# The first W1 quarter ahead of phi, keys, values and queries, and one order for the first softmax, the first VW and the first W2 chunks

## The chip, the cores and the metric

The kernel runs on one core of one Trainium2 chip. The metric is the device time of one execution in microseconds (us); a smaller time is better. The kernel before was timed in three runs.

## The reference

Three stages follow each other, all in float32, over 8 batches of 576 rows and 512 columns. An attention over 32 memory slots per head comes first, then a layer norm with a two-layer network of 2048 hidden columns, then a second gated network. The weights of the first network, `w_ch1` (W1) and `w_ch2` (W2), arrive as float64 words.

```python
a = softmax(phi, axis=2)                                   # 8 batches, 8 heads, 576 rows, 32 slots
k_m = np.einsum('bhsm,bhsd->bhmd', a, k)                   # head_dim 64
v_m = np.einsum('bhsm,bhsd->bhmd', a, v)
attn = softmax(q @ k_m.transpose(0, 1, 3, 2) / sqrt(64))
x = heads_side_by_side(attn @ v_m)                         # (8, 576, 512)
xn = (x - mean(x)) / sqrt(var(x) + 1e-6) * g_ln
x = x + np.maximum(xn @ w_ch1, 0.0) @ w_ch2                # (512, 2048), (2048, 512)
h = gelu(x @ w_in)                                         # (512, 1024)
u, v = h[..., :512], h[..., 512:]
v_s = np.einsum('ts,bsd->btd', w_sg, layernorm(v) * g_ln2) + b_sg[None, :, None]
out = x + (u * v_s) @ w_out
```

## The kernel before, in words

**The products.** Since x is attn @ v_m, the kernel never forms xn @ W1. It multiplies v_m with W1 once per batch and quarter of W1 (`make_vw`, the tiles `pvw` in PSUM) and then multiplies the attention weights with that (`m1`, the products `ph`). The layer norm is taken in by scaling W1 with g_ln (`scale_w1`) and taking off its column mean (`center_w1`: four products `cm` with a constant column, then two subtractions on VectorE); the division by the deviation comes at the end. Every float32 operand of `m1` and `m2` is held as a high and a low part, so that a product is three passes. `evict_vw` writes the high part of VW on ScalarE and the low part on VectorE.

**The stages at the head.** W1 is taken in four quarters of 512 columns, four raw tiles each; W2 in sixteen chunks of 128 rows. A raw tile of W1 or W2 is turned from float64 to float32 by `to_f32`, with one instruction on ScalarE (L112) and two on VectorE (L113, L114). `split_w2` then casts the high part on ScalarE (L126) and subtracts the low part on GpSimd (L127). For batch 0 phi, keys and values become the means `kvp` (`prep_max`, `prep_exp`, `prep_sum`, `prep_kv`), which are divided by their sums (`ptsum`, `rs`, `kvn`) and turned (`prep_T`, the tile `kvT`). The queries are turned on TensorE (`t_q`, the tiles `ptq`). The scores `sc` of the 576 rows are taken in three groups: two tiles of 128 rows, two more, and the last 64 rows. `t_scores`, `t_norm` and `t_attn` are their softmax; the last writes its high and low parts, `aTh` and `aTl`. `m1` of the first block of 256 rows needs group 0, `m1` of the second block of 320 rows needs groups 1 and 2. `m2` multiplies the hidden rows with a W2 chunk into the tiles `py`.

**The order.** Every piece of work stands in one list with a time (`at_time(time, function, ...)`); `run_until` records them by that time. From there a scheduler gives each engine its own order, which the engine keeps on the chip, whatever arrives late. `tc.issue_after(ins)` holds an instruction behind another in that order. All loads go through one queue (SP, `load`, L85), with at most eight on the way.

**PSUM at the head.** `ps_0` hands out four banks y0 to y3 in turn, to `pt`, `mb`, `cm`, `ptq`, `ptsum`, `ptk` and the scores of batch 0; the tiles `py` of row tiles 0 to 3 use the same four, tile n the bank yn. In the order of the list the scores of group 2 take y1 and y2. `ps_a` has two more banks, for `kvp`, `px` and, from quarter 1 on, `cm` and `pvw`.

## Time and profile before

| | us |
|---|---|
| median of three runs | 1208.05 (1207.62 to 1212.12) |
| the profiled execution's own time | 1207.83 |
| its span in the profile | 1206.0 |
| TensorE busy | 1167.4 |
| VectorE busy | 689.7 |
| ScalarE busy | 467.1 |
| GpSimd busy | 400.7 |

Busy times are sums over instructions. Times in a trace count from the start of the span; the profiled execution's own time is 1.83 us longer than its span. TensorE products follow each other in a pipeline, so that a sum of their durations counts more than the engine needs.

### The profile page before, as it was taken

To read this page: it belongs to the slowest core of one execution; us is meant where nothing else is said; L and a number is where in the kernel's file an instruction comes from. 1 tells how busy PE (TensorE), PEld (TensorE's weight loads), DVE (VectorE), ACT (ScalarE), POOL (GpSimd) and SP (SyncE) were. 2 spreads that over 40 slices of the span, in tenths; PEclk is the share of its full clock that TensorE was granted. 3 is DMA by queue.
4 is the path that set the end of the run, shared out by engine and by line. 5 is a ranking of instruction groups with operands and counts; after the bars stand their busy time and mean duration, and the time that the engine had idled before them with its cause. 6 is when DMAs were issued, how large, how long until landed. Compare 5 with 4: busy or idle time off the path is not lost.

```text
span 1206.0 us, 20725 instructions
## 1 busy us (share of the span) xinstructions
PE 1167.4 (97%) x7711; PEld 991.3 (82%) x7711; DVE 689.7 (57%) x1669; ACT 467.1 (39%) x1071; POOL 400.7 (33%) x622
## 2 busy tenths in 40 slices
PE   4699999999999999999999999999999999999998
PEld 2377678888788888788888888889989988998997
DVE  2887665755645545644645445568576477447532
ACT  3575333332432322332323445445444354344430
POOL 2133212211201211201211112456666475566641
PEclk9699999999999999999999999999999999999999
DMA  8996744373341443331410343122240042022201
GB/s 205 284 287 177 219 106 125 79 205 66 109 117 31 129 137 66 97 107 23 128 36 27 106 118 115 35 82 88 77 143 18 19 142 77 1 81 86 79 18 70
DMA packets 199141, 124.15 MB, mean 103 GB/s; under 512 B 93312, under 2 KB 174336, under 8 KB 199040
## 3 DMA queue, kind: packets, MB, share of 16 engines
q1 hardware_dynamic: 199040, 122.82, 36.4%
q8 instruction: 61, 1.00, 0.3%
q14 instruction: 40, 0.33, 0.1%
HBM read 99.72 MB, written 31.33 MB: 109 GB/s over the span
## 4 chain that ended last, share of the span: by engine, by line
PE 86%; DVE 5%; DMA 4%; SPq 2%; issue 1%; POOL 1%; ACT 1%; POOLq 0%; DVEq 0%
PE ph L592 16%; PE py L622 10%; PE py L624 10%; PE py L623 10%; PE pvs L1027 8%; PE po L1050 8%; PE pv L918 8%; PE pu L1002 7%; PE pvw L544 2%; DMA raw<-in_moe_w_ch_dram 2%; SPq L85 2%; PE kvp L315 1%; DMA q<-q_d 1%; PE cm L504 1%; PE sc L401 1%
## 5 line engine op out<-in xcount | busy, mean ns | idle before, releaser
L592 PE MATMUL ph<-aTh,vw 128*128 128x320 f32 (+1 forms) x1024 | 247.2, 300 | 3.5 <-ACT aTh L440 1.4
L622 PE MATMUL py<-whl,hh 128*128 128x512 f32 x512 | 201.8, 396 | 3.0 <-ACT hh L578 3.0
L592 PEld LDWEIGHTS ph<-aTh,vw 128*128 128x128 f32 x1024 | 178.2, 190 | 28.3 <-issue 9.4
L623 PE MATMUL py<-whl,hh 128*128 128x512 f32 x512 | 201.3, 393 | 0.0
L624 PE MATMUL py<-whl,hl 128*128 128x512 f32 x512 | 183.2, 397 | 0.0
L578 ACT ACTIVATE hh<-ph 128x256 fp32r<-128x256 f32 x256 | 96.6, 385 | 167.7 <-PE ph L592 111.5
L579 DVE SCALAR_TENSOR_TENSOR hl<-ph,hh 128x256 fp32r<-128x256 f32 x256 | 106.5, 421 | 87.6 <-ACT hh L578 87.0
L592 PE MATMUL ph<-aTl,vw 128*128 128x256 f32 (+1 forms) x512 | 152.2, 297 | 0.0
L1027 PE MATMUL pvs<-wsh,vhl 128*128 128x288 f32 x576 | 121.0, 295 | 0.0
L622 PEld LDWEIGHTS py<-whl,hh 128*128 128x128 f32 x512 | 96.3, 188 | 26.9 <-ACT hh L578 5.7
L623 PEld LDWEIGHTS py<-whl,hh 128*128 128x128 f32 x512 | 96.5, 189 | 19.3 <-issue 0.8
L1002 PE MATMUL pu<-yTh,whl 128*128 128x288 f32 x512 | 111.0, 296 | 0.3 <-DVE ug L907 0.3
L592 PEld LDWEIGHTS ph<-aTl,vw 128*128 128x128 f32 x512 | 97.1, 190 | 10.3 <-issue 2.9
L624 PEld LDWEIGHTS py<-whl,hl 128*128 128x128 f32 x512 | 89.9, 189 | 12.0 <-issue 2.3
L1027 PEld LDWEIGHTS pvs<-wsh,vhl 128*128 128x128 f32 x576 | 94.4, 188 | 0.6
L918 PE MATMUL pv<-whl,yTh 128*128 128x512 f32 x288 | 91.0, 396 | 0.0
L1050 PE MATMUL po<-whl,gh 128*128 128x512 f32 x288 | 90.0, 391 | 0.0
L1002 PEld LDWEIGHTS pu<-yTh,whl 128*128 128x128 f32 x512 | 85.4, 189 | 1.8 <-DVE ug L907 0.8
L578 ACT ACTIVATE cr<-ph 128x64 fp32r<-128x64 f32 x128 | 28.6, 226 | 130.7 <-PE ph L592 130.1
L1030 POOL TENSOR_TENSOR gt<-gt,ug 128x288 f32<-128x288 f32 x64 | 52.8, 826 | 68.5 <-DVE gt L1029 62.1
L1027 PE MATMUL pvs<-wsl,vhl 128*128 128x288 f32 x256 | 75.6, 295 | 0.0
L1002 PE MATMUL pu<-yTl,whl 128*128 128x288 f32 x256 | 75.5, 295 | 0.0
(154 smaller groups left out, 2162.4 us busy)
## 6 DMA issues: line engine op xcount, KB each, us to landing
wc<-w_d SPq DMA_DIRECT2D x28, 512.0 KB, 6.0
y_d<-x SPq DMA_DIRECT2D x36, 256.0 KB, 2.3
yt<-y_d SPq DMA_DIRECT2D x36, 256.0 KB, 2.7
yr<-y_d SPq DMA_DIRECT2D x36, 256.0 KB, 2.8
kv<-in_k_dram SPq DMA_DIRECT2D x32, 256.0 KB, 3.6
kv<-in_v_dram SPq DMA_DIRECT2D x32, 256.0 KB, 4.0
raw<-in_moe_w_ch_dram SPq DMA_DIRECT2D x32, 256.0 KB, 8.5
raw<-in_moe_w_ch_dram SPq DMA_DIRECT2D x16, 512.0 KB, 6.1
```

The lines of the kernel that those rows point to most:

```text
L85: return nc.sync.dma_start(out=out_ap, in_=in_ap)
L578: high = A.activation(out_h, src, AF.Relu)
L579: return high, V.scalar_tensor_tensor(out=out_l, in0=src, scalar=0.0, in1=out_h.bitcast(F32), op0=ALU.max, op1=ALU.subtract)
L592: R["ph"] = PE.matmul(ph, w_[:, ks], x[:, g, 0:w], start=(n == 0), stop=(n == 3 * HK - 1))
L622: PE.matmul(py, hh, wh, start=start, stop=False)
L623: PE.matmul(py, hh, wl, start=False, stop=False)
L624: PE.matmul(py, hl, wh, start=False, stop=stop)
L918: PE.matmul(pv, y[:, kc, cs], w, start=(n == 0), stop=(n == 3 * KC - 1))
L1002: PE.matmul(pu, w[:, ds_], y[:, kc, cs], start=(n == 0), stop=(n == 3 * KC - 1))
L1027: PE.matmul(pvs, v_, w_, start=(n == 0), stop=(n == len(ops) - 1))
L1030: G.tensor_tensor(out=gt, in0=gt, in1=ug, op=ALU.mult)
L1050: PE.matmul(po, gg[:, dc, cs], w, start=(n == 0), stop=(n == 3 * KC - 1))
```

## The change

Seven things move, all before the orders of the two kernels meet again on TensorE, some 130 us into the program.

1. The first W1 quarter is loaded first of all, with g_ln (`g1c`) between its halves; `g2c` is loaded later. It is scaled and centred at once, at list times -29 and -28 instead of -16.5 and -16.4.
2. The queries of group 0 are loaded behind phi, ahead of keys and values; those of groups 1 and 2 still behind them.
3. W2 chunks 0 to 3 are loaded ahead of W1 quarter 1, chunks 4 and 5 ahead of quarter 2.
4. `make_vw` of quarter 0 stands ahead of the scores, and its banks come from `ps_a`.
5. Groups 0, 1 and 2 of the first softmax stand one behind the other, with W2 chunk 0 behind group 0, chunk 1 in group 1, chunks 2 and 3 at group 2. Gates hold this order on VectorE and ScalarE.
6. The conversions of W1 quarters 1 to 3 are chained: each waits for the word conversion before it, and quarters 2 and 3 also for the last centring and scaling.
7. W2 chunks 4 to 7 wait behind the last eviction of VW.

```diff
+    def behind(gate):
+        es = ExitStack()
+        for ins in gate or ():
+            es.enter_context(tc.issue_after(ins.ins))
+        return es
...
-    def split(raws, wp, scale=None, gate=None):
+    def split(raws, wp, scale=None, gate=None, late=None):
...
-                A.copy(h, w)
+                with behind(late):
+                    A.copy(h, w)
...
-            with tc.issue_after(st["kvT", b][1].ins):
+            with behind([R["evicted"][0] if b == 0 else st["kvT", b][1]]):
...
-            for g in range(2):
-                V.transpose(out=z[:, g * w:(g + 1) * w], in_=sc[g])
+            with behind(gr.get("gate")):
+                for g in range(2):
+                    V.transpose(out=z[:, g * w:(g + 1) * w], in_=sc[g])
...
-            V.tensor_reduce(out=r, in_=z3, axis=AX.X, op=ALU.add)
+            with behind(gr.get("gate")):
+                V.tensor_reduce(out=r, in_=z3, axis=AX.X, op=ALU.add)
...
+                    if fb + j == 0:
+                        load(g1c[64 * g:64 * g + 64, :], g1[g * 4 * D:(g + 1) * 4 * D].rearrange("(c p) -> p c", p=D))
...
-                w = to_f32(raw, [st.get("hl", tiles[TB - 1]["tr"])] if fb else None)
-                A.activation(d, w, AF.Copy, scale=g1c[:, j:j + 1])
+                gate = [R["word"]] if j + fb else []
+                if fb:
+                    gate += [st["hl"], st["centred"], st["scaled"]] if "hl" in st else [first_grs[2]["ah"]]
+                w = to_f32(raw, gate)
+                st["scaled"] = A.activation(d, w, AF.Copy, scale=g1c[:, j:j + 1])
...
-                    ps = [ps_of(b + turn, [P, DM], "pvw") for _ in range(HK)]
+                    ps = [ps_a.tile([P, DM], F32, tag="a", name="pvw") for _ in range(HK)]
...
-            for ps, (h, l) in zip(st.pop(("vw", b, turn)), VW[b, TURNS[b % 2][turn]]):
-                A.copy(h, ps)
-                V.tensor_tensor(out=l, in0=ps, in1=h.bitcast(F32), op=ALU.subtract)
+            with behind([first_grs[0]["exp"], first_grs[0]["tr"]] if b + turn == 0 else None):
+                for ps, (h, l) in zip(st.pop(("vw", b, turn)), VW[b, TURNS[b % 2][turn]]):
+                    high = A.copy(h, ps)
+                    R["evicted"] = high, V.tensor_tensor(out=l, in0=ps, in1=h.bitcast(F32), op=ALU.subtract)
...
-            gate = st.get("hl", tiles[1 if c == 0 else 3]["tr"])
-            W2[c] = split([raws.pop(("w2", c))], wpool, gate=[gate])
+            gate = [st["hl"], *(R["evicted"] if c < 8 else ())] if "hl" in st else [st.get("turn", R["evicted"][1]), st.get("act", R["evicted"][0])]
+            late = [first_grs[0]["ah"]] if c == 0 else None
+            W2[c] = split([raws.pop(("w2", c))], wpool, gate=gate, late=late)
+            if c < 3:
+                first_grs[1 + c // 2]["gate"] = [R["word"]]
...
-                        at_time(-27, load_q, us[i], ub, qi)
+                        at_time(-33.3 if gi == 0 else -27, load_q, us[i], ub, qi)
...
-                    at_time(-17 + 0.1 * tt, t_scores, gr)
-                    at_time(-16 + 0.1 * tt, t_norm, gr)
-                    at_time(-16 + 0.1 * tt, t_attn, gr)
+                    at_time((-17.4, -16.2, -15.5)[gi], t_scores, gr)
+                    at_time((-17.3, -15.9, -15.3)[gi], t_norm, gr)
+                    at_time((-17.2, -15.7, -15.2)[gi], t_attn, gr)
...
-            at_time((-26.5, -26.2, -2.5, 2.0)[fb], load_w1, fb)
-            at_time((-16.5, -5.0, 3.0, 7.5)[fb], scale_w1, fb)
-            at_time((-16.4, -0.3, 4.6, 9.1)[fb], center_w1, fb)
-            at_time((-15, 1.3, 5.8, 10.3)[fb], make_vw, 0, [fb])
-            at_time((-15, 1.3, 5.8, 10.3)[fb], evict_vw, 0, fb)
+            at_time((-34, -25.7, -2.5, 2.0)[fb], load_w1, fb)
+            at_time((-29, -5.0, 3.0, 7.5)[fb], scale_w1, fb)
+            at_time((-28, -0.3, 4.6, 9.1)[fb], center_w1, fb)
+            at_time((-17.5, 1.3, 5.8, 10.3)[fb], make_vw, 0, [fb])
+            at_time((-17, 1.3, 5.8, 10.3)[fb], evict_vw, 0, fb)
...
-            split_at = 4.5 * (c // 4) + 0.5625 * (c % 4) - 0.6 if c > 3 else 0.9 * c - 4
-            at_time(split_at - 5 if c > 3 else -12.7 if c == 3 else 0.2 * c - 26.4, load_w2, c)
+            split_at = 4.5 * (c // 4) + 0.5625 * (c % 4) - 0.6 if c > 3 else (-16.8, -16.0, -15.6, -15.4)[c]
+            at_time(split_at - 5 if c > 5 else 0.1 * c - 3.2 if c > 3 else 0.2 * c - 26.4, load_w2, c)
```

TensorE at the head of the program, from its first product, before. `pt` and `mb` belong to phi, `kvp` to keys and values, `ptsum` to the sums, `ptq` to the queries (q_209 group 0, q_214 group 1).

```order
L258 MATMUL pt<-ident,pm 128x128 x2
L270 MATMUL mb<-dg,mcol 128x128 x2
L315 MATMUL kvp<-kv,phi 32x128 x16
L315 MATMUL kvp<-kvr,prz 32x128 x4
L315 MATMUL kvp<-kv,phi 32x128 x8
L297 MATMUL ptsum<-ident,sm 128x128
L315 MATMUL kvp<-kv,phi 32x128 x8
L315 MATMUL kvp<-kvr,prz 32x128 x4
L297 MATMUL ptsum<-ident,sm 128x128
L376 MATMUL ptq<-ident,q_209 128x128 x8
L376 MATMUL ptq<-ident,q_214 128x128 x4
L352 MATMUL ptk<-ident,kvn 128x128 x2
```

The same place now; q_173 are the queries of group 0, q_250 those of group 1, q_255 those of group 2, and the two latter are the last loads of batch 0.

```order
L262 MATMUL pt<-ident,pm 128x128
L524 MATMUL cm<-wc,mcol 128x512 x4
L262 MATMUL pt<-ident,pm 128x128
L274 MATMUL mb<-dg,mcol 128x128
L380 MATMUL ptq<-ident,q_173 128x128 x4
L380 MATMUL ptq<-ident,q_250 128x128 x4
L274 MATMUL mb<-dg,mcol 128x128
L319 MATMUL kvp<-kv,phi 32x128 x16
L319 MATMUL kvp<-kvr,prz 32x128 x4
L380 MATMUL ptq<-ident,q_255 128x64 x4
L380 MATMUL ptq<-ident,q_173 128x128 x4
L319 MATMUL kvp<-kv,phi 32x128 x16
```

The centring of W1 and a turn of group 1's queries have moved in front of the second `mb`, which phi's second half needs, and all of `kvp` stands behind them.

VectorE around group 0's softmax, before; z_358, z_375 and z_392 are the scores of groups 0, 1 and 2.

```order
L424 TENSOR_TENSOR z_358<-z_358,r_424 128x512
L429 STREAM_TRANSPOSE z_358<-z_358 128x512
L421 TENSOR_REDUCE r_434<-z_375 128x16
L113 TENSOR_SCALAR raw<-raw 128x512
L422 TENSOR_SCALAR r_434<-r_434 128x16
L506 TENSOR_TENSOR wc<-wc,cm 128x1024 x2
L423 RECIPROCAL r_434<-r_434 128x16
L114 SCALAR_TENSOR_TENSOR raw<-raw 128x512
L424 TENSOR_TENSOR z_375<-z_375,r_434 128x512
L429 STREAM_TRANSPOSE z_375<-z_375 128x512
```

The same place now; z_398 and z_435 are the scores of groups 0 and 1.

```order
L434 TENSOR_TENSOR z_398<-z_398,r_405 128x512
L439 STREAM_TRANSPOSE z_398<-z_398 128x512
L572 TENSOR_TENSOR vw<-pvw,vw 128x512 x2
L116 TENSOR_SCALAR raw<-raw 128x512
L117 SCALAR_TENSOR_TENSOR raw<-raw 128x512
L415 STREAM_TRANSPOSE z_435<-sc 128x256 x2
L418 TENSOR_REDUCE m_438<-z_435 128x16
L603 SCALAR_TENSOR_TENSOR hl<-ph,hh 128x256
L419 TENSOR_TENSOR z_435<-z_435,m_438 128x512
L116 TENSOR_SCALAR raw<-raw 128x512
L603 SCALAR_TENSOR_TENSOR hl<-ph,hh 128x256
L117 SCALAR_TENSOR_TENSOR raw<-raw 128x512
```

Group 1's transposes and maximum, which stood ahead of group 0's exponent, now stand behind VW and W2 chunk 0, and low parts of the hidden rows (`hl`) stand between them.

ScalarE at the eviction of VW of quarter 1, before; raw_508 and its like are W1, `px` is attn @ v_m.

```order
L550 CAST vw<-pvw 128x512 x2
L112 ACTIVATE raw<-raw 128x512
L578 ACTIVATE cr<-ph 128x64
L112 ACTIVATE raw<-raw 128x512
L578 ACTIVATE cr<-ph 128x64
L578 ACTIVATE hh<-ph 128x256 x2
L498 ACTIVATE wc<-raw_508,g1c 128x512
L498 ACTIVATE wc<-raw_511,g1c 128x512
```

The same place now:

```order
L571 CAST vw<-pvw 128x512 x2
L115 ACTIVATE raw<-raw 128x512 x4
L518 ACTIVATE wc<-raw_528,g1c 128x512
L115 ACTIVATE raw_531<-raw_531 128x512
L475 COPY x<-px 128x512
L130 CAST whl<-raw 128x512
L475 COPY x<-px 128x512
L602 ACTIVATE hh<-ph 128x256 x2
```

The copy of `px`, which gives a `ps_a` bank back to the next `cm`, now stands behind four W2 conversions and a scaling of W1.

## Rows read from the trace of the kernel before

**Rows 1.** The page, part 1: busy us, share, instructions of each engine.

```profile
PE 1167.4 (97%) x7711; PEld 991.3 (82%) x7711; DVE 689.7 (57%) x1669; ACT 467.1 (39%) x1071; POOL 400.7 (33%) x622
```

**Rows 2.** Windows: stretch, length, busy us PE, PEld, DVE, ACT, POOL; PEclk, DMA share, GB/s.

```profile
25.00:35.00 10.00, 0.78 (x27) 0.21 (x9) 5.24 (x11) 5.38 (x8) 0.00 (x0) 0.63 1.02 240
50.00:55.00 5.00, 4.74 (x16) 3.62 (x16) 5.00 (x14) 1.43 (x4) 0.67 (x1) 0.51 1.03 246
62.50:80.00 17.50, 17.50 (x107) 14.41 (x107) 15.12 (x33) 14.32 (x32) 5.39 (x5) 1.00 1.05 341
100.00:125.00 25.00, 24.10 (x184) 18.14 (x184) 16.61 (x36) 11.73 (x28) 11.01 (x10) 1.00 0.57 159
```

**Rows 3.** The chain that ended last, at the head: start us, us, what.

```profile
26.03 8.97 DMA raw<-in_moe_w_ch_dram
...
43.51 7.71 DMA raw<-in_moe_w_ch_dram
```

**Rows 4.** Timeline, phi, keys and values: start us, us, engine, line, [idle before <-releaser].

```profile
2.86 1.05 SPq L85 DMA_DIRECT2D phi<-in_phi_dram  x2
...
10.55 0.69 DVE L271 TENSOR_TENSOR phi<-phi,mb 128x512 f32<-128x512 f32 x1 [0.17 <-PE mb L270]
...
15.19 0.98 POOL L288 TENSOR_TENSOR sm<-sm,prz 64x128 f32<-64x128 f32 x2
...
17.34 1.08 PE L315 MATMUL kvp<-kv,phi 128*32 128x128 f32 x16 [1.17 <-DMA kv<-in_v_dram]
...
18.78 0.48 PE L297 MATMUL ptsum<-ident,sm 128*128 128x128 f32 x1
...
22.06 0.37 ACT L354 COPY kvT<-ptk 128x256 f32<-128x256 f32 x1
```

**Rows 5.** Timeline, ScalarE taking W1 and W2 tiles as they land, first and fifth.

```profile
30.52 0.68 ACT L112 ACTIVATE raw<-raw 128x512 f32<-128x512 f32 x1 [1.43 <-DMA raw<-in_moe_w_ch_dram]
...
39.16 0.67 ACT L112 ACTIVATE raw<-raw 128x512 f32<-128x512 f32 x1 [1.46 <-DMA raw<-in_moe_w_ch_dram]
```

**Rows 6.** Timeline, from the first centring to the second block's first product.

```profile
35.42 6.55 PE L504 MATMUL cm<-wc,mcol 128*128 128x512 f32 x8
...
44.54 2.35 DVE L506 TENSOR_TENSOR wc<-wc,cm 128x1024 f32<-128x1024 f32 x2
...
45.81 3.06 PE L544 MATMUL pvw<-wc,kvT 64*32 64x512 f32 x16 [3.85 <-DVE wc L506]
...
49.82 0.58 PE L592 MATMUL ph<-aTh,vw 128*128 128x256 f32 x1 [0.95 <-ACT vw L550]
...
62.57 0.31 PE L592 MATMUL ph<-aTh,vw 128*128 128x320 f32 x1
```

**Rows 7.** Groups of VectorE, then ScalarE, 22 to 50 us: busy us, mean ns | idle before.

```profile
L114 DVE SCALAR_TENSOR_TENSOR raw<-raw 128x512 uint32<-128x512 uint32 x5 | 3.4, 680 | 1.1 <-ACT raw L112 1.1
...
L113 DVE TENSOR_SCALAR raw<-raw 128x512 uint32<-128x512 uint32 x5 | 2.1, 426 | 7.8 <-DMA raw<-in_moe_w_ch_dram 7.8
L410 DVE STREAM_TRANSPOSE z<-sc 128x256 f32<-128x256 f32 x4 | 1.4, 416 | 0.0
L429 DVE STREAM_TRANSPOSE z<-z 128x512 f32<-128x512 f32 x2 | 1.4, 712 | 0.1
L424 DVE TENSOR_TENSOR z<-z,r 128x512 f32<-128x512 f32 x2 | 1.4, 682 | 0.0
...
L421 DVE TENSOR_REDUCE r<-z 128x16 f32<-128x512 f32 x2 | 1.3, 665 | 2.6 <-ACT z L415 2.6
...
L415 ACT ACTIVATE z<-z 128x512 f32<-128x512 f32 x2 | 1.2, 612 | 0.0
```

**Rows 8.** The chain that ended last, two W2 products at the full clock.

```profile
58.51 0.47 PE py L624 x2
```

**Rows 9.** Timeline, a low part of W2 on GpSimd and a word shift on VectorE.

```profile
78.90 1.31 POOL L127 TENSOR_TENSOR whl<-raw,whl 128x512 fp32r<-128x512 f32 x1
...
79.15 1.34 DVE L113 TENSOR_SCALAR raw<-raw 128x512 uint32<-128x512 uint32 x1
```

More of the change, by code (lines that the diff above doesn't have):

```diff
@@ L439, in t_attn @@
                 ah, al = (x[:, :, c0:c0 + m] for x in aT_of(j))
-                A.copy(ah, src)
+                gr["ah"] = A.copy(ah, src)
                 lo = (V if 0 < t0 <= TB and b == 0 else G).tensor_tensor(out=al, in0=src, in1=ah.bitcast(F32), op=ALU.subtract)
+            gr["tr"] = tr
+            if b == 0:
+                st["act"] = gr["ah"]
+                if gr is not first_grs[0]:
+                    st["turn"] = tr
             for u in us:
@@ L534, in make_vw @@
                 runs.append((fb, ps))
-            claims = [V.memset(t[:, 0:2], 0.0).ins.name for _, ps in runs for t in ps] if b + turns[0] else []
+            claims = [V.memset(t[:, 0:2], 0.0).ins.name for _, ps in runs for t in ps]
             for fb, _ in runs:
@@ L817, in load_bias @@
         R["bb"] = bb = R["p2"].tile([P, NW], F32, name="bb", bufs=1)
+        load(g2c, g2.rearrange("(c p) -> p c", p=P))
         load(bb[:, REM:NW], b_sg.unsqueeze(0).to_broadcast([P, S]))
@@ L1088, in phase2 @@
         es_right.close()
-    for g in range(2):
-        load(g1c[64 * g:64 * g + 64, :], g1[g * 4 * D:(g + 1) * 4 * D].rearrange("(c p) -> p c", p=D))
-    load(g2c, g2.rearrange("(c p) -> p c", p=P))
     phase1()
```

20 lines of the change are left out of this document (12 added, 8 removed).

## The prediction

> **What bounds the kernel now.** I read the page's busy shares first: TensorE has work in 97% of the span and no other engine in more than 57% [rows 1]. Little can be won in the middle, and the windows say where it is not dense: from 25 to 35 us TensorE is busy for 0.8 us of 10, from 50 to 55 us it works at a granted clock of 0.51, which is the lower of its two levels (1.2 GHz), after an idle stretch, and from 62.5 us on it has no gap until some 0.9 us are lost between 100 and 125 us [rows 2]. The chain of waits tells what the head waits for: from 26 us on it is the landing of W1 and W2 tiles, until 51 us [rows 3]. The timeline then gives the path: keys and values are in at 17.3 us and the turned means `kvT` are ready at 22.4 [rows 4], but the first product of the network, `ph`, starts at 49.8, because the tiles of the first W1 quarter land only after them [rows 3], its centring took 6.6 us of TensorE at the lower level and 2.4 us of VectorE, and `pvw` had to wait for it [rows 6]. The change takes this quarter off that path. The orders of the two kernels differ only up to about 130 us on TensorE, and the same products stand between the first `ph` and that point, so the difference of the times is the shift of the first `ph` plus what TensorE loses behind it, now against before.
>
> The sum is made against the profiled execution, 1207.83 us; the median of the runs stands 0.2 above it. A measurement of this kernel can tell about 0.5%, or 6 us, from no change.
>
> **Term 1, the first `ph`.** The load of phi is the fourth issue and stands at 2.86 us [rows 4]; the first stands at about 0.7, so the queue starts 2.1 us earlier. Four tiles of 512 KB land in 39.16 - 30.52 = 8.6 us [rows 5], which is what phi, keys and values now wait for. The queries of group 0 (another 512 KB, at the same rate 2.2 us) go ahead of the keys too. So the last keys land at 17.3 - 2.1 + 8.6 + 2.2 = 26.0 us, and the first half of group 1's queries 1.1 us later, at 27.1. This is where it matters that TensorE's order now has a turn of these queries in front of the second `mb` and of every `kvp`: TensorE stands there until 27.1. From there: four transposes and the `mb` 1.6 us to the subtraction in phi; before, the second such subtraction began 0.8 us after the first at 10.55, and GpSimd's sums ended at 16.2, 4.8 us later [rows 4]. Sums therefore at 33.5. TensorE meanwhile has both groups of `kvp`, 2 x 2.4 us (16 of 40 passes take 1.08 [rows 4]), and three turns, and is through at about 34.3. From `ptsum` to the end of `kvT` it took 3.7 us before, some of it behind a turn of the queries [rows 4]; I take 3.0. `kvT` at 37.3; since TensorE works on end from 27 us on it may be back at its upper level, which would give 36. I take 36.8.
>
> Then `pvw`, for which before shows 3.1 us at the lower level with a wait in it [rows 6] and which takes half at the upper: 1.5. Scores 0.8. Group 0's softmax in a chain: transposes 0.7, maximum and subtraction 1.3, exponent 0.6, sum 0.7, two short steps 0.4, product 0.7, transpose 0.7, cast 0.6 [rows 7], with the hops 6.2. First `ph` at 36.8 + 1.5 + 0.8 + 6.2 = 45.3, **4.5 us earlier** than 49.8. Bounds: 42.8 if the loads keep the 1.5 us better and TensorE its upper level, 48 if both go the other way.
>
> **Term 2, from the first `ph` to the second block.** Before, the first product of 320 columns came at 62.57, 12.8 us behind the first `ph` [rows 6], and groups 1 and 2 of the softmax were mostly done by then, since VectorE had them while TensorE centred W1. Now they stand behind VW and between W2 chunks. VectorE's list from group 0's last transpose to group 2's low part: two VW low parts 1.4, the words of four W2 chunks and one of W1 4.9, group 1 5.2, group 2 2.6, four low parts of hidden rows 1.7: 15.8 us at the durations of [rows 7]. Instructions that don't depend on each other overlap by some 0.07, 25 times: -1.7. It waits for ScalarE and TensorE (the exponent stands behind two `hh`, and these behind products at the lower level): +2.6. One meeting with GpSimd: before, a word shift that takes 0.43 elsewhere took 1.34 beside a low part of W2 on GpSimd, and ended behind it [rows 9]: +0.9. That is 17.6 us, which begins 0.7 before the first `ph`. TensorE itself is bound to about the same time: `py` of tile 1 needs the bank y1, which holds scores of group 2 until VectorE has turned them, some 13.5 us into that list; 14 products of 0.23 us at the upper level [rows 8] or twice that at the lower stand between, and TensorE will have been idle, so I take the lower for most: 5 us. So 17.5 instead of 12.8: **+4.7**. By then TensorE has done 12 more W2 products than before at that place (2.8 us) and 6 `px` (0.7) and the centring of quarter 1 (half of 6.55) less: **+1.2** still to do.
>
> The Trainium skill (SBUF — State Buffer, Who interferes with whom) says that VectorE and GpSimd share a port pair, and that an instruction that needs it blocks the other engine's wholly, whichever came first; the trace agrees at this one place [rows 9]. By that rule every such meeting costs what [rows 9] show, and the sum would be that of the first rival below.
>
> **Term 3, from there to where the orders meet.** VectorE still owes the words of quarter 1 (three tiles and a half, 3.9), its centring 2.4 and a few more, where before it had done them. I follow it: centred some 12.5 us behind the second block's start, `pvw` then, low parts of VW 1 us later than TensorE would take them; and the first `cm` of quarter 2 needs the bank of `px`, whose copy on ScalarE stands behind four W2 conversions: 1.2 more. With small waits 2.7, against the 0.9 before [rows 2]: **+1.8**.
>
> W2 tiles land earlier relative to their use, and the later load of `g2c` and the chained gates cost nothing as long as TensorE, full from 62.5 us, hides them; without that cover the chain would show as term 3 again, at each quarter.
>
> **Sum.** -4.5 + 4.7 + 1.2 + 1.8 = +3.2: 1211.0 in the terms of the profiled execution, 1211.3 beside the median. That is 0.3%, within what counts as no change. By the bounds of term 1 (-7 to -1.8) and of term 2 (VectorE without any wait, +2; all at the lower level, +7) its own range is 1206 to 1215.
>
> **Rivals.** *More meetings with GpSimd.* GpSimd has eight low parts of W2 of 1.3 us and four of the values to do while VectorE does two-operand and word instructions on end; each meeting costs 0.9 [rows 9] and I counted one. Five more on the path give 1211.3 + 4.5 = 1215.8; from four on it is slower by over 0.5%. For it: VectorE is the limit in this stretch and the softmax is full of such instructions. Against: most low parts follow a cast, at times when VectorE may be in transposes. The rule of the Trainium skill on the port pair stands beside this one: chance 0.20.
>
> *TensorE waits at each quarter.* What term 3 finds once (a bank of `ps_a` that comes free behind ScalarE's conversions) could come at quarters 2 and 3 again, 2 us each: 1215.3. For it: the order was set for other arrival times than these. Against: before, TensorE loses only 0.9 us there. Chance 0.15.
>
> *The head is faster than I follow it.* If the queries don't hold TensorE and the keys land at 24, `kvT` stands 5.1 later [rows 4], at 29.1, `ph` at 38 (-11.8); with VectorE's list at its bare 14 us (+1.2), +1.2 still to do and +1 for term 3 the time is 1207.8 - 8.4 = 1199.4. It decides at a first `ph` before 40. Against: the bytes ahead of the keys. Chance 0.13.
>
> *Nothing moves.* The gain at the head and the softmax behind it cancel, or transfers share the engines so that phi lands as before and W1 no earlier: 1208. Chance 0.05.
>
> **Numbers.** My forecast has 0.47. Faster by over 0.5%: 0.13, the third rival. Slower: 0.20 + 0.15 = 0.35. Within: 0.47 + 0.05 = 0.52. The range, 1203 to 1218, takes in both slower rivals with some spread and leaves the third out.
>
> **What would show it.** The first `cm` before 25 us; TensorE idle until about 27 us and then the turn of group 1's queries; `kvT` near 37; first `ph` near 45; VectorE without gaps from there to 62, `py` of tile 1 waiting for a VectorE transpose; the first product of 320 columns near 63. A first `ph` before 41, or a second block before 58, would prove me wrong on the side of faster; word shifts of 1.3 us in that stretch, or a wait of several us for `px` at each quarter, on the other.

## The result and the profile after

The changed kernel takes 1217.24 us (median of six runs, 1215.57 to 1218.60), the kernel before 1208.37 in six runs beside them: a ratio of 1.0067 with a 95% interval of 1.0048 to 1.0085. That is 0.67% slower. The profiled execution took 1216.79, with a span of 1215.0 against 1206.0.

Page of the changed kernel, part 1 (it answers to [rows 1]):

```profile
PE 1167.7 (96%) x7711; PEld 990.2 (82%) x7711; DVE 695.8 (57%) x1671; ACT 467.5 (38%) x1071; POOL 402.1 (33%) x622
```

TensorE is busy for 0.3 us more; the other 8.7 of the 9.0 us of span are time in which it stands idle. Windows of the changed kernel, with the columns of [rows 2], say where:

```profile
25.00:35.00 10.00, 6.25 (x104) 4.61 (x104) 4.16 (x12) 3.83 (x9) 3.09 (x5) 1.00 0.96 299
40.00:50.00 10.00, 3.96 (x26) 3.08 (x21) 8.96 (x17) 5.06 (x12) 4.37 (x6) 0.63 1.05 274
50.00:55.00 5.00, 3.75 (x16) 3.08 (x15) 3.97 (x10) 2.65 (x6) 0.62 (x2) 0.71 0.93 220
55.00:62.50 7.50, 4.20 (x10) 2.75 (x10) 6.99 (x13) 2.73 (x5) 2.35 (x2) 0.59 0.60 160
62.50:80.00 17.50, 17.13 (x88) 12.25 (x88) 12.19 (x31) 10.39 (x23) 1.31 (x1) 0.98 0.77 222
80.00:100.00 20.00, 18.98 (x112) 14.11 (x110) 19.06 (x44) 14.79 (x30) 9.22 (x14) 1.00 0.88 238
100.00:125.00 25.00, 22.24 (x149) 16.18 (x141) 19.93 (x38) 16.28 (x34) 9.93 (x9) 1.00 0.73 210
```

The same stretch from 40 to 62.5 us in the kernel before, as one window:

```profile
40.00:62.50 22.50, 16.53 (x66) 9.17 (x65) 20.49 (x48) 14.06 (x27) 4.24 (x4) 0.75 1.03 314
```

The hole at 25 to 35 us is filled (6.25 busy us instead of 0.78), and another has grown from 40 to 62.5: 11.9 busy us of 22.5 instead of 16.5, at granted clocks of 0.59 to 0.71, while VectorE is busy for 19.9. From 62.5 to 125 TensorE now loses 4.2 us where it lost 0.9.

TensorE's timeline in the changed kernel, the landmarks that answer to [rows 4] and [rows 6] (start us, us, engine, line, [idle before <-releaser]):

```profile
17.63 5.94 PE L524 MATMUL cm<-wc,mcol 128*128 128x512 f32 x8 [0.77 <-DVE mx L264]
23.40 0.27 PE L262 MATMUL pt<-ident,pm 128*128 128x128 f32 x1
...
27.64 0.63 PE L380 MATMUL ptq<-ident,q 128*128 128x128 f32 x4 [0.77 <-DMA q<-in_q_dram]
28.10 0.39 PE L274 MATMUL mb<-dg,mcol 128*128 128x128 f32 x2
...
36.34 1.96 PE L564 MATMUL pvw<-wc,kvT 64*32 64x512 f32 x16 [0.46 <-ACT kvT L358]
...
45.80 0.79 PE L616 MATMUL ph<-aTh,vw 128*128 128x256 f32 x2 [5.40 <-ACT aTh L450]
...
59.49 0.80 PE L646 MATMUL py<-whl,hh 128*128 128x512 f32 x1 [2.43 <-DVE z L415]
...
64.50 0.46 PE L616 MATMUL ph<-aTh,vw 128*128 128x320 f32 x2
...
84.88 1.98 PE L524 MATMUL cm<-wc,mcol 128*128 128x512 f32 x4 [0.56 <-ACT x L475]
108.45 0.36 PE L616 MATMUL ph<-aTh,vw 128*128 128x256 f32 x1 [1.81 <-DVE hl L603]
...
137.98 0.38 PE L356 MATMUL ptk<-ident,kvn 128*128 128x128 f32 x2
```

The last row is the turn of batch 1's means, near which the orders of the two kernels meet; before it stood here:

```profile
130.03 0.38 PE L352 MATMUL ptk<-ident,kvn 128*128 128x128 f32 x2
```

The first `ph` is 4.0 us earlier than in [rows 6]. The first product of 320 columns stands 18.7 behind it instead of 12.75, and `ptk` another 73.5 behind that instead of 67.5. So the shift at `ptk` is -4.0 + 5.95 + 6.0 = +7.95 us, and 1.0 more comes between there and the end.

### The profile page after: what moved, and what is told of

Read it like the earlier page. It is cut to its first block, busy times and chain, and to the rows that moved or that the text cites. A ratio compares the mean times of both kernels' runs of the same rounds, so it can differ in the third digit from the quotient of the medians.

```text
span 1215.0 us, 20733 instructions
## 1 busy us (share of the span) xinstructions
PE 1167.7 (96%) x7711; PEld 990.2 (82%) x7711; DVE 695.8 (57%) x1671; ACT 467.5 (38%) x1071; POOL 402.1 (33%) x622
## 4 chain that ended last, share of the span: by engine, by line
PE 85%; DVE 6%; DMA 3%; issue 2%; ACT 2%; POOL 1%; SPq 1%; POOLq 0%; DVEq 0%; ACTq 0%
PE ph L616 16%; PE py L646 10%; PE py L648 10%; PE py L647 10%; PE pvs L1055 8%; PE po L1078 8%; PE pv L946 8%; PE pu L1030 7%; PE pvw L564 2%; PE kvp L319 1%; DMA q<-q_d 1%; PE sc L405 1%; SPq L85 1%; PE px L474 1%; PE px L473 1%
```

## The experiments

All twelve were timed beside the kernel before; ratios are to it, with 95% intervals. The last three columns are read from TensorE's timeline: the first `ph`, the distance from it to the first product of 320 columns, and `ptk` of batch 1.

| kernel | median us | ratio | first `ph` | to 320 columns | `ptk` |
|---|---|---|---|---|---|
| before | 1208.37 | | 49.82 | 12.75 | 130.03 |
| the change | 1217.24 | 1.0067 (1.0048 to 1.0085) | 45.80 | 18.70 | 137.98 |
| e1_no_chain | 1219.39 | 1.0088 (1.0067 to 1.0109) | 50.80 | 24.29 | 140.89 |
| e2_no_low | 1214.23 | 1.0046 (1.0033 to 1.0059) | 43.43 | 18.62 | 134.31 |
| e3_banks | 1216.70 | 1.0062 (1.0039 to 1.0085) | 44.58 | 17.85 | 137.91 |
| e4_w2_early | 1213.65 | 1.0038 (1.0025 to 1.0051) | 47.62 | 10.43 | 135.88 |
| e5_item1 | 1209.66 | 1.0011 (0.9999 to 1.0024) | 49.21 | 13.17 | 130.99 |
| e6_early_act | 1215.59 | 1.0051 (1.0032 to 1.0070) | 47.00 | 10.65 | 135.67 |
| e7_act_gate | 1215.68 | 1.0057 (1.0036 to 1.0078) | 44.36 | 18.76 | 136.80 |
| e8_cm_behind | 1207.80 | 0.9990 (0.9979 to 1.0001) | 37.96 | 18.56 | 128.86 |
| e9_sub_behind | 1212.42 | 1.0036 (1.0023 to 1.0050) | 42.32 | 18.51 | 133.19 |
| e10_combined | 1209.42 | 1.0007 (0.9996 to 1.0017) | 38.24 | 17.73 | 131.51 |
| e11_item1_cm | 1207.92 | 0.9996 (0.9986 to 1.0007) | 40.17 | 21.15 | 128.72 |
| e12_order | 1208.96 | 1.0005 (0.9991 to 1.0019) | 39.59 | 16.95 | 130.07 |

One profile's landmarks are good to 1 or 2 us: `pvw` starts at 36.34 in the change and at 35.31 in e1, whose order is the same up to there. About a microsecond of this is the change's own profile: its first `cm` starts at 17.63, those of e1, e3, e7 and e9 between 16.5 and 17.0, with the same order ahead of it. The medians of e1, e2, e3, e6 and e7 differ from the change's by 0.5 to 3 us, with intervals that overlap with its interval; those of e4 and e9 just touch it, and the others lie clear of it.

### The gates: e1 and e7

Items 6 and 7 were undone in e1.

```diff
-                gate = [R["word"]] if j + fb else []
-                if fb:
-                    gate += [st["hl"], st["centred"], st["scaled"]] if "hl" in st else [first_grs[2]["ah"]]
+                gate = [st.get("hl", tiles[TB - 1]["tr"])] if fb else []
...
-            gate = [st["hl"], *(R["evicted"] if c < 8 else ())] if "hl" in st else [st.get("turn", R["evicted"][1]), st.get("act", R["evicted"][0])]
+            gate = [st["hl"]] if "hl" in st else [st.get("turn", R["evicted"][1]), st.get("act", R["evicted"][0])]
```

> Items 6 and 7 alone undone: W1 quarters 1 to 3 and W2 chunks 4 to 7 wait for a hidden row's low part only, as before the change. Theory A (VectorE's list is the bound between 43 and about 115 us, whatever holds its order; it owes the words of W1 quarter 1 and of the W2 chunks, which before were done by then): the same work stays on VectorE, first ph at 45.8, 320-column ph at 64 to 65, total within 2 us of the changed kernel's 1217.2. Theory B (the chained gates make TensorE wait at each quarter): TensorE's idle time between 75 and 125 us falls from 4 us to 1, total 1213 to 1214. Theory C (port meetings of VectorE and GpSimd): no change that can be told.

Its median is 2.2 us above the change's. The waits of the change at the later quarters are mostly gone: from 75 to 125 us three waits of 0.36, 0.27 and 0.47 us are left, and from the 320 columns to `ptk` it takes 65.8 us instead of 73.5. Of these 7.7 us, 5.4 are busy time of TensorE, since the centring of quarter 1 and six `px` now stand ahead of the 320 columns, and 2.3 are waits. The conversion of W1 quarter 1 has moved forward. ScalarE takes its four tiles ahead of group 0's exponent (L422) and waits for the landing of each; VectorE takes them between groups 1 and 2. ScalarE in e1, then VectorE:

```profile
39.38 0.67 ACT L115 ACTIVATE raw<-raw 128x512 f32<-128x512 f32 x1 [4.12 <-DMA raw<-in_moe_w_ch_dram]
...
46.52 0.61 ACT L422 ACTIVATE z<-z 128x512 f32<-128x512 f32 x1
```

```profile
47.17 0.69 DVE L431 TENSOR_REDUCE r<-z 128x16 f32<-128x512 f32 x1 [6.72 <-ACT z L422]
...
64.40 3.10 DVE L117 SCALAR_TENSOR_TENSOR raw<-raw 128x512 uint32<-128x512 uint32 x5
```

VectorE waits 6.72 us for the exponent, where it waits 0.69 in the change. The first `ph` stands at 50.80 and the 320 columns 24.3 behind it. So the gates move a debt of VectorE and ScalarE, the conversion of W1 quarter 1, behind the second block. Whether they also cost waits of their own at the later quarters is not shown, because e1 takes away the gates and the debt at once.

In e7 the gate of W2 chunks 4 to 15 holds ScalarE as well, so that the copies of `px` don't stand behind conversions.

```diff
-            gate = [st["hl"], *(R["evicted"] if c < 8 else ())] if "hl" in st else [st.get("turn", R["evicted"][1]), st.get("act", R["evicted"][0])]
+            gate = [*R["relu"], *(R["evicted"] if c < 8 else ())] if "hl" in st else [st.get("turn", R["evicted"][1]), st.get("act", R["evicted"][0])]
```

> The changed kernel with the gate on ScalarE's part of the conversions of W2 chunks 4 to 15 alone, so that the copy of px no longer stands behind four of them. Term 3 as the prediction had it (the first cm of quarter 2 needs the bank of px, 1.2 us): the waits in front of px and cm at 81.7 and 84.9 us go (1.0 us together), total 1215.5 to 1216.5. Theory A (VectorE's debt is term 3): the waits for hl and VW between 100 and 115 us stay, total within 1 us of 1217.2.

The wait of `cm` for `px` is gone, and others have its place. TensorE in e7, later in the same stretch:

```profile
106.30 0.50 PE L646 MATMUL py<-whl,hh 128*128 128x512 f32 x1 [1.40 <-ACT hh L602]
...
114.54 0.41 PE L616 MATMUL ph<-aTh,vw 128*128 128x320 f32 x1 [1.15 <-DVE hl L603]
```

From the 320 columns to `ptk` it takes 73.7 us, as in the change; the 1.6 us in the median are less than these runs can tell. Taking the wait for the bank of `px` away does not shorten the stretch.

### Behind the first `ph`: e2, e3, e4, e6

VectorE in the change: a short step without a neighbour, and then five instructions that take longer than elsewhere, each beside a GpSimd instruction, with two between them that don't:

```profile
42.89 0.17 DVE L432 TENSOR_SCALAR r<-r 128x16 f32<-128x16 f32 x1
...
46.19 1.25 DVE L116 TENSOR_SCALAR raw<-raw 128x512 uint32<-128x512 uint32 x1
...
48.97 0.69 DVE L418 TENSOR_REDUCE m<-z 128x16 f32<-128x512 f32 x1
...
49.90 0.98 DVE L419 TENSOR_TENSOR z<-z,m 128x512 f32<-128x512 f32 x1
50.80 0.42 DVE L116 TENSOR_SCALAR raw<-raw 128x512 uint32<-128x512 uint32 x1
...
54.96 1.59 DVE L434 TENSOR_TENSOR z<-z,r 128x512 f32<-128x512 f32 x1
...
60.13 1.54 DVE L116 TENSOR_SCALAR raw<-raw 128x512 uint32<-128x512 uint32 x1
...
64.12 0.79 DVE L451 TENSOR_TENSOR aTl<-z,aTh 128x128 fp32r<-128x128 f32 x1 [0.36 <-ACT aTh L450]
```

GpSimd in the change, beside them:

```profile
45.89 1.27 POOL L451 TENSOR_TENSOR aTl<-z,aTh 128x512 fp32r<-128x512 f32 x1 [0.18 <-ACT aTh L450]
49.03 1.30 POOL L131 TENSOR_TENSOR whl<-raw,whl 128x512 fp32r<-128x512 f32 x1 [1.87 <-ACT whl L130]
54.71 1.29 POOL L131 TENSOR_TENSOR whl<-raw,whl 128x512 fp32r<-128x512 f32 x1 [4.38 <-ACT whl L130]
60.04 1.35 POOL L131 TENSOR_TENSOR whl<-raw,whl 128x512 fp32r<-128x512 f32 x1 [4.04 <-ACT whl L130]
63.44 1.31 POOL L131 TENSOR_TENSOR whl<-raw,whl 128x512 fp32r<-128x512 f32 x1 [2.06 <-ACT whl L130]
```

The word shift takes 0.42 at 50.80 and 1.25 and 1.54 in the meetings. The product of a softmax (L434) takes 0.68 in the kernel before [rows 7]; the subtraction (L419) and the last low part (L451, 128x128) take 0.68 and 0.29 in e2 below, where GpSimd's instruction beside them is left out. So the five meetings cost 0.83 + 0.30 + 0.90 + 1.12 + 0.50 = 3.65 us. Each ends 0.16 to 0.55 us behind GpSimd's instruction, whenever it began.

In e2 GpSimd's low parts of W2 chunks 0 to 3 are left out, and TensorE reads the high part twice in their place; its result lacks these low parts.

```diff
-                G.tensor_tensor(out=l, in0=w, in1=h.bitcast(F32), op=ALU.subtract)
+                if low:
+                    G.tensor_tensor(out=l, in0=w, in1=h.bitcast(F32), op=ALU.subtract)
...
+            W2[c] = split([raws.pop(("w2", c))], wpool, gate=gate, late=late, low=c > 3)
```

> GpSimd's four low parts of W2 chunks 0 to 3 are left out; TensorE reads the high part a second time in their place, so its work is the same. Four instructions of 1.3 us go from GpSimd at 49.0, 54.7, 60.0 and 63.4 us, beside which VectorE took 0.98, 1.59 and 1.54 us for what takes 0.69, 0.68 and 0.42 alone (2.3 us together). Theory C (port meetings are what makes VectorE's list long): 320-column ph 2 to 2.5 us earlier, near 62.2, total 1214.5 to 1215.5. Theory A (the length of the list itself, 15 to 16 us of work behind the first ph): it gains the same 2.3 us at most at that place, and less in the end, since the debt of W1 quarter 1 stays: 1215 to 1217. Theory D (TensorE is held by bank y1 and by the W2 parts, not by VectorE): under 1 us at the 320-column ph, 1216.5 to 1217.5.

VectorE's list ends 16.3 us behind the first `ph` instead of 19.1, about what the four meetings cost. The median is 3.0 us below the change's, but the gain does not lie in this stretch: the profile has the first `ph` 2.4 us earlier and 1.2 less between the 320 columns and `ptk`, while the 320 columns still come 18.6 behind the first `ph`. Of the 2.4 us, 1.1 are there already at `pvw`, and the rest is `pvw` and the scores at the upper level of the clock (granted 0.98 from 36 to 40 us, 0.59 in the change); the edit does nothing yet at that place, so that this part is not its work. TensorE in e2 shows why the stretch stays as long:

```profile
55.65 0.80 PE L647 MATMUL py<-whl,hh 128*128 128x512 f32 x1 [2.94 <-DVE z L416]
56.25 0.63 PE L648 MATMUL py<-whl,hh 128*128 128x512 f32 x1
56.67 0.63 PE L649 MATMUL py<-whl,hl 128*128 128x512 f32 x1
```

`py` of tile 1 waits for its bank, and the products behind the wait start 0.43 apart, at the lower level, where they take 0.23 at the upper one [rows 8]. This wait ends 12.2 us behind the first `ph` instead of 13.7, but from there to the 320 columns it takes 6.4 us instead of 5.0, because more of the products run at the lower level. So there are two bounds at one place. The other one was taken away in e3, which hands the scores of batch 0 the next bank in turn.

```diff
-            sc = [ps_of(b, [P, w], "sc") for _ in range(2)]
+            st["ps0"] += b == 0 and gr is first_grs[0]; sc = [ps_of(b, [P, w], "sc") for _ in range(2)]
```

> The rotation of the four banks is moved on by one ahead of the scores of batch 0, so that group 2's scores stand in y2 and y3 and py of row tile 1 (bank y1) no longer waits for group 2's transposes, only for group 1's at 48.2 us. Theory D (the bank is what holds TensorE until 59.5 us): the wait of 2.4 us in front of py goes, 320-column ph near 62, total 1214.5 to 1215.5. Theory A (VectorE's list ends at 64.9 us with group 2's low part, which the 320-column products need): py comes earlier, the 320-column ph stays between 63.5 and 65 and TensorE waits there for aTh or aTl of group 2 instead; total 1216 to 1218.

There, too, hardly anything is won (0.5 us in the median): the wait in front of `py` is for W2's cast now. TensorE in e3:

```profile
58.02 0.73 PE L646 MATMUL py<-whl,hh 128*128 128x512 f32 x2 [2.77 <-ACT whl L130]
```

Neither bound alone gives the stretch back. A third way takes work out of it: VectorE stood idle for 5.48, 4.24 and 3.78 us at three places between 18 and 39 us, and e4 puts the W2 conversions there, chunk 0 ahead of `rs` and 1 to 3 behind `kvn`, with no gates in the softmax (`st["norm"]` is the last of `kvn`). e6 is e4 with the later chunks gated on ScalarE as well, as in e7.

```diff
-            gate = [st["hl"], *(R["evicted"] if c < 8 else ())] if "hl" in st else [st.get("turn", R["evicted"][1]), st.get("act", R["evicted"][0])]
-            late = [first_grs[0]["ah"]] if c == 0 else None
-            W2[c] = split([raws.pop(("w2", c))], wpool, gate=gate, late=late)
-            if c < 3:
-                first_grs[1 + c // 2]["gate"] = [R["word"]]
+            gate = [st["hl"], *(R["evicted"] if c < 8 else ())] if "hl" in st else [st["norm"]] if c else None
+            W2[c] = split([raws.pop(("w2", c))], wpool, gate=gate)
...
-            split_at = 4.5 * (c // 4) + 0.5625 * (c % 4) - 0.6 if c > 3 else (-16.8, -16.0, -15.6, -15.4)[c]
+            split_at = 4.5 * (c // 4) + 0.5625 * (c % 4) - 0.6 if c > 3 else -17.9 if c else -22
```

> The gates that hold the conversion of W2 chunks 0 to 3 behind the first VW and inside the softmax are taken out: chunk 0 is converted ahead of the sums' reciprocal, chunks 1 to 3 behind the division by the sums, in the stretches of 4.2 us (from 29.5) and 3.8 us (from 35.5) in which VectorE stands idle; groups 1 and 2 of the softmax lose their gates too. Everything else as changed. Theory A (VectorE's list behind the first ph is the bound): its four conversions (4.4 us) and three meetings with GpSimd (2.3 us) leave that list; first ph 45.5 to 47, 320-column ph 58 to 60, total 1209 to 1212, and below 1208 only if the debt of W1 quarter 1 goes as well. Theory B (the chained gates of quarters 1 to 3 cost the time): the waits between 75 and 125 us stay, total 1213 to 1215. Rival: the chunks land too late (after 34 us) and hold the reciprocal and the division behind them on VectorE: first ph at 48 or later, total 1216 to 1219.

> As the run with W2 chunks 0 to 3 converted early (1213.65), and ScalarE's part of the later conversions is now held too: the gates of W2 chunks 4 to 15 name ScalarE's last hidden row beside VectorE's. In that run ScalarE took up chunk 8 at 75.50 after a wait of 2.57 us for its landing, the hidden row hh stood behind it, TensorE waited 3.37 us and worked at the lower clock for 5 us after. If that wait is what kept its gain: 3.4 us of idle time and some 2.5 us of half clock go, total 1207.5 to 1209. If VectorE still owes its work at that place (words of quarters 1 and 2, 75 to 100 us), the wait turns into one for VW or hl and less than 2 us come back: 1212 to 1213.5.

The stretch behind the first `ph` falls to 10.4 us in e4 and 10.7 in e6, shorter than in the kernel before. So what made it long was the conversion of four W2 chunks in it, with the gates that held the softmax behind them. Yet of these 8 us only 3.6 reach the median of e4, and 1.6 that of e6. The first `ph` itself stands 1.8 and 1.2 us later, since VectorE has the conversions ahead of it, and the rest comes back as waits for landings. ScalarE in e4, then VectorE in e6:

```profile
75.50 0.65 ACT L115 ACTIVATE raw<-raw 128x512 f32<-128x512 f32 x1 [2.57 <-DMA raw<-in_moe_w_ch_dram]
```

```profile
94.79 0.45 DVE L383 STREAM_TRANSPOSE qT<-q 128x256 f32<-128x256 f32 x1 [4.87 <-DMA q<-q_d]
```

In e4 a later W2 chunk, not yet landed, is taken by ScalarE ahead of a hidden row's high part, and `py` stands 3.4 us behind it. In e6 VectorE reaches a turn of batch 1's queries, which have not landed, and low parts of the hidden rows stand behind it.

### The head: e5, e8, e9

The kernel before with item 1 alone is e5: W1's first quarter is loaded in front, `g2c` later, scaled and centred at once (the two small loads moved as in the change, not shown).

```diff
-            at_time((-26.5, -26.2, -2.5, 2.0)[fb], load_w1, fb)
-            at_time((-16.5, -5.0, 3.0, 7.5)[fb], scale_w1, fb)
-            at_time((-16.4, -0.3, 4.6, 9.1)[fb], center_w1, fb)
+            at_time((-34, -26.2, -2.5, 2.0)[fb], load_w1, fb)
+            at_time((-29, -5.0, 3.0, 7.5)[fb], scale_w1, fb)
+            at_time((-28, -0.3, 4.6, 9.1)[fb], center_w1, fb)
```

> The kernel before with item 1 alone: the first W1 quarter with g_ln is loaded first, scaled and centred at once, and g2c is loaded later; loads of queries, W2 and quarter 1, the softmax, VW and all gates as before the change. Theory A (behind the first ph VectorE's list is the bound, and it holds the same work in either order): the gain at the first ph is lost again behind it as in the changed kernel, 1211 to 1217. Theory E (item 1 alone is the gain of 4 us and the rest, the order of items 2 to 7, gives it away): first ph at 45 to 47, 320-column ph 12.8 later, total 1203 to 1206. Rival: with the loads in the old order W1 quarter 1 and W2 chunks are taken up by ScalarE before they have landed, and kvT, the exponent or VW stand behind them: first ph at 48 or later, 1210 to 1216.

It is the same as before (0.11% above, in an interval that takes in no change), and its first `ph` is only 0.6 us earlier. TensorE in e5:

```profile
39.71 2.47 PE L401 MATMUL sc<-qT,kvT 64*32 64x256 f32 x48 [5.35 <-ACT kvT L354]
```

The copy of `kvT` on ScalarE stands behind the conversions of W1 quarter 1, which wait for landings. Items 3, 5 and 6, which put quarter 1 behind W2 and hold it, take that wait away in the change. So item 1 alone neither gains nor loses. It already brings one thing that e8 and e9 find costly in the change: `cm` and a turn of group 1's queries stand in front of the second `mb`, at 26.58 in e5.

The other two take the changed kernel and undo its hold on phi (the diffs are e8's and then e9's; `st["mb"]` and `st["psub"]`, set in lines not shown, are the `mb` of phi and the subtraction behind it). In the change `cm` stands between the two halves of phi on TensorE (17.63 to 23.4), the subtraction between them on VectorE (23.61, 2.35 us), and a turn of group 1's queries in front of the second `mb`. In e8 `cm` stands behind the second `mb` (the scheduler then puts that turn behind too); in e9 `cm` stays, and the subtraction and the turns go behind.

```diff
-                PE.matmul(cm, mean, ws[j // 2][:, j % 2, :], start=(j == 0), stop=(j == KC - 1))
+                with behind([] if fb else [st["mb"]]): PE.matmul(cm, mean, ws[j // 2][:, j % 2, :], start=(j == 0), stop=(j == KC - 1))
```

```diff
-                    PE.transpose(pt[:, c, :], t[:, c].rearrange("p o d -> p (o d)"), ident[:n, :n])
+                    with behind([] if gr is first_grs[0] else [st["mb"]]): PE.transpose(pt[:, c, :], t[:, c].rearrange("p o d -> p (o d)"), ident[:n, :n])
...
-                st["centred"] = V.tensor_tensor(out=ws[n], in0=ws[n], in1=cm.unsqueeze(1).to_broadcast([P, 2, DM]), op=ALU.subtract)
+                with behind([] if fb else [st["psub"]]): st["centred"] = V.tensor_tensor(out=ws[n], in0=ws[n], in1=cm.unsqueeze(1).to_broadcast([P, 2, DM]), op=ALU.subtract)
```

> The changed kernel with the first centring's products (cm) held behind the second mb in TensorE's order, so that phi's subtraction and exponent come before the centring and no turn of group 1's queries stands in front of them. GpSimd's sums then end near 25 us instead of 33.4 and the means wait for the last keys alone: kvT at 30 to 33 instead of 36.3, first ph at 40 to 43. Theory A (VectorE's list behind the first ph is the bound): the list starts 3 to 5 us earlier, but W2 chunks 0 and 1, landing at 31 to 33 us, stand in it as before; 320-column ph 60 to 62, total 1213 to 1215. Theory F (from 60 us on the transfers and the debt set the time, the start of the list does not): the gain at the first ph is gone by 130 us, total 1216 to 1217.5. Rival: the centring, now later, is waited for by pvw: first ph not before 45.

> The changed kernel with the products of the first centring (cm, 4.4 to 5.9 us on TensorE) left in front of phi's second maximum, but with the centring's subtraction on VectorE (2.35 us) behind phi's second subtraction and the turns of groups 1 and 2 behind the second mb. It splits the 9.4 us that holding cm behind mb gave. Theory G (what was queued behind cm on VectorE and TensorE, the subtraction of 2.35 and the turn of group 1 that waits for its queries until 27.6 us, is what held phi): kvT 3.5 to 4.5 us earlier than 36.3, first ph near 41.5, total 1212.5 to 1214, and the rest of the 9.4 is cm itself. Theory H (cm alone is the cost): kvT and total within 1.5 us of the changed kernel. Theory I (the turn that waits for the queries, as the prediction named it, is nearly all): total under 1210.

TensorE in e8:

```profile
19.37 0.64 PE L274 MATMUL mb<-dg,mcol 128*128 128x128 f32 x2
19.80 4.36 PE L524 MATMUL cm<-wc,mcol 128*128 128x512 f32 x8
...
29.79 1.09 PE L564 MATMUL pvw<-wc,kvT 64*32 64x512 f32 x16 [0.43 <-ACT kvT L358]
...
37.96 0.80 PE L616 MATMUL ph<-aTh,vw 128*128 128x256 f32 x2 [5.40 <-ACT aTh L450]
...
51.25 0.79 PE L646 MATMUL py<-whl,hh 128*128 128x512 f32 x1 [3.40 <-DVE z L415]
```

The second `mb` comes 8.7 us earlier than in the change, `pvw` 6.6, the first `ph` 7.8, and the kernel is 9.4 us faster than the change by the medians. In e9 the first `ph` comes 3.5 earlier and 4.8 reach the end. So under the order of the change an early head is passed on about one to one: the stretch behind it keeps its 18.6 us. And e8 is no faster than the kernel before, although its first `ph` is 11.9 us earlier: what stands behind the first `ph` costs it nearly as much, 5.8 us up to the 320 columns and 4.9 from there to `ptk`.

### Versions meant to beat both: e10, e11, e12

e8, e3 and e7 together are e10 (their three edits, as above).

> The changed kernel with cm behind the second mb, the banks turned on by one and ScalarE's part of the W2 conversions gated, the three edits that gave 9.4, 0.5 and 1.5 us when made alone. If they add up: 1205.5 to 1206.5, under the kernel before by 0.1 to 0.2%. If the transfers of W1 quarters 2 and 3 and of batch 1's queries are the bound by then (waits for a landing between 75 and 100 us): 1207 to 1208.5.

The small gains don't add up: it is 1.6 us above e8.

e11 leaves the order of the kernel before and takes item 1, `cm` behind the second `mb`, and ScalarE's conversions of W1 quarter 1 and W2 chunks 1 to 3 behind group 0's `aTh`. e12 adds the loads of item 3, moves quarter 1 behind group 2's `aTh` and gates the later conversions on ScalarE.

```diff
-                w = to_f32(raw, [st.get("hl", tiles[TB - 1]["tr"])] if fb else None)
+                w = to_f32(raw, [st.get("hl", tiles[TB - 1]["tr"])] + [st["ah0"]] * (fb == 1) if fb else None)
...
-                PE.matmul(cm, mean, ws[j // 2][:, j % 2, :], start=(j == 0), stop=(j == KC - 1))
+                with tc.issue_after(st["mb"].ins) if fb == 0 else ExitStack():
+                    PE.matmul(cm, mean, ws[j // 2][:, j % 2, :], start=(j == 0), stop=(j == KC - 1))
...
-            W2[c] = split([raws.pop(("w2", c))], wpool, gate=[gate])
+            W2[c] = split([raws.pop(("w2", c))], wpool, gate=[gate, st["ah0"]] if 0 < c < 4 else [gate])
```

> The kernel before with item 1 (first W1 quarter loaded, scaled and centred first), with cm held behind the second mb, and with ScalarE's part of W1 quarter 1 and of W2 chunks 1 to 3 held behind the cast of group 0's attention weights (aTh), so that neither kvT nor the exponent stands behind a landing; softmax, VW and W2 stand in the order of the kernel before. Theory A (the changed order of softmax, VW and W2 is what makes VectorE's list behind the first ph 18.6 us long where it was 12.8): first ph at 37 to 40, 320-column ph 12.5 to 14 later, at 50 to 54, total 1199 to 1203, faster than before by 0.4 to 0.7%. Theory F (the transfers set the time from 60 us on): the gain at 320 columns is lost in waits for landings before 110 us, total 1206 to 1208.

> The kernel before with four parts: item 1, cm held behind the second mb, item 3 (W2 chunks 0 to 3 loaded ahead of W1 quarter 1, chunks 4 and 5 ahead of quarter 2), and gates on ScalarE: W2 chunks 1 to 3 behind group 0's aTh, W1 quarter 1 behind group 2's aTh, all later conversions behind the last hidden row. The softmax of the three groups stands interleaved as before the change. In the run with item 1 and cm alone, ScalarE waited 0.5 and 2.3 us for chunks 2 and 3 at 43.5 and 46.5 us with the hidden rows behind it, and TensorE stood 4.4 us. Theory A (what makes the stretch behind the first ph long is VectorE's list and the landings that stand in it, both of which this order avoids): first ph at 39 to 41, 320-column ph at 50 to 54, total 1199 to 1203, faster than before by 0.4 to 0.7%. Theory F (an earlier head only moves the wait to later landings, of W1 quarter 2 or batch 1's queries, before 110 us): waits of 4 us or more there, total 1206 to 1208.5.

Both are the same as before. e11 has its first `ph` 9.65 us earlier and spends 8.4 of it behind that: ScalarE waits for W2 chunks to land, and hidden rows stand behind the waits. In e12 batch 1's queries bind, as in e6. ScalarE in e11, then VectorE in e12:

```profile
46.46 0.65 ACT L112 ACTIVATE raw<-raw 128x512 f32<-128x512 f32 x1 [2.32 <-DMA raw<-in_moe_w_ch_dram]
...
48.07 0.65 ACT L583 ACTIVATE hh<-ph 128x256 fp32r<-128x256 f32 x2
```

```profile
97.91 0.45 DVE L379 STREAM_TRANSPOSE qT<-q 128x256 f32<-128x256 f32 x1 [3.90 <-DMA q<-q_d]
```

With a first `ph` anywhere from 37.96 to 49.82, `ptk` comes at 128.7 to 131.5 in all of before, e5, e8, e10, e11 and e12, never earlier. Landings bind in e4, e6, e11 and e12. In e8 TensorE's waits between the 320 columns and `ptk` come to 2.6 us, each of 1.2 or less; what else keeps it from going below was not settled, and no version tried beats the kernel before.

## Why the prediction was right or wrong

The likeliest case, 1211.3 and within what counts as no change, was 5.9 us too low. The range (1203 to 1218) held the time, and the side of the two slower rivals came true. The sum was -4.5 + 4.7 + 1.2 + 1.8 = +3.2; it came out as -4.0 + 5.95 + 1.6 + 4.4 + 1.0 = +9.0 between the profiled executions. (The prediction's own range of 1206 to 1215 should end at 1216 by the bounds it names: -1.8 + 7 + 1.2 + 1.8 = +8.2.)

**Term 1, right in size, in part by luck.** The first `ph` stands at 45.80 (forecast 45.3), the first `cm` at 17.63 (before 25 us), the second `mb` at 28.10, `pvw` at 36.34 (forecast 36.8). The turn of group 1's queries did wait for its landing in front of the second `mb`, until 27.64 (forecast 27.1). What the step left out is that `cm` and the subtraction held phi's second half to almost the same time: `mx` of that half ran at 25.87 and its `mb` could not have started before 27.1. So two holds ended within 1 us of each other, and only one was forecast. e8, which takes both away, shows what they cost: 7.8 us of the head. The term was taken as the price of the bytes ahead of the keys; the order on TensorE and VectorE was at least as large a part.

**Term 2, mechanism right, size off: +5.95 instead of +4.7.** VectorE had a list to 64.9 with 1.7 us of waits in it, `py` of tile 1 waited for a transpose of the scores, and the 320 columns came at 64.5 (forecast 63). The term that was mis-sized is the meetings with GpSimd, counted once at 0.9: there were five, 3.65 us. The waits within the list were 1.7 where 2.6 were taken, and the list's own work 14.6 against 14.1, so the list is 19.9 us long against 17.6. e4 and e6, which take the W2 conversions out of it, bring the stretch to 10.4 and 10.7 us. That TensorE is bound to about the same time, by the bank and the lower clock, was put into the forecast as a remark; e2 and e3 show that it is a second full bound.

The Trainium skill (SBUF — State Buffer, Who interferes with whom) says that on trn2 a `tensor_reduce` never contends for the port pair, while an operation with both inputs in SBUF does. The trace agrees: the reduction at 48.97 takes 0.69 us, as such a reduction does without a neighbour (0.665 in [rows 7]), beside the GpSimd instruction that lengthens the subtraction at 49.90 to 0.98; that instruction, which began 0.06 us behind the reduction, takes its usual 1.30.

**Work owed, about +1.6 instead of +1.2.** The forecast's counts hold in the traces: ahead of the 320 columns stand 12 more W2 products, no `px` where there were six, and no centring of quarter 1. At the spacings behind 64.5 us in the change this is, as an estimate, 3.6 for the centring (forecast 3.3) and 0.7 for `px`, less 2.8 for the W2 products.

**Term 3, the step that failed: +4.4 instead of +1.8.** From the 320 columns to `ptk` the change takes 73.5 us against 67.5, of which about 1.6 is the work owed. TensorE's waits there come to 4.1 us against 0.9, so 3.2 of the 4.4 are idle time; the other 1.2 lie where it shows as busy, and what they are stays open. The forecast put the loss on the bank of `px` (1.2 us); that wait is 0.56, and e7 removes it without shortening the stretch. The largest wait is 1.81 for `hl` on VectorE, which is busy for 19.1 of the 20 us from 80 to 100. e1 speaks for a debt behind it: without the gates quarter 1 is converted ahead of the 320 columns, and the waits behind them fall from 4.1 to 1.8 us. That the debt and not the gates of the later quarters makes the waits is argued, not shown. The follow-up of VectorE's list in the forecast stopped one quarter too soon.

**The last 1.0.** Behind `ptk` the change takes 1077.0 us and before 1076.0. Except e11 (1079.6), the other kernels lie between 1075.9 and 1077.5, so this is within what single profiles scatter.

**The rivals.** *More meetings with GpSimd* (1215.8, chance 0.20) is what the rows show: four meetings too many, 2.75 us of the list. e2, without the low parts, has a median 3.0 us lower, though the stretch itself stays as long and part of the gain stands in front of it. *TensorE waits at each quarter* (1215.3, chance 0.15) came true in sum, 4.1 us of waits, mostly not by the bank that it named. Each alone came within 2 us of the time, but in the runs they came together, and the forecast's own case had neither in full. *The head is faster* needed a first `ph` before 40. e8 has it, at 37.96, and still takes 1207.8 and not 1199.4: the stretch behind it, put at 14 us there, is 18.6, and from the 320 columns to `ptk` it takes 4.9 us more than before, where 2.2 were put. *Nothing moves* is excluded by the landmarks.

## What to carry to other kernels

Moving a load forward moves its processing forward too, into the queues of engines on the path: here the centring stood between two halves of phi, and one line that put it behind them was worth 9.4 us in the changed kernel. When work is moved out of an idle stretch, follow the engine that does it until its debt is paid, and count its meetings with GpSimd one by one. Where two bounds end at the same time, taking one away can show nothing; take work out of the stretch instead, and look for the next landing.
